# Attention and a two-axis DFT on one core: right operands in four pieces, x terms in three cycles, five weight sets during V

## The chip, the cores and the metric

The kernel runs on one core of one Trainium2 chip. The metric is the device time in microseconds of one execution. TensorE (PE) multiplies, VectorE (DVE), ScalarE (ACT) and GpSimd (POOL) work on tiles, and SyncE (SP) issues nearly all the DMA transfers, in the order of its own queue.

## The reference

The input x has 2048 rows of 640 numbers. One branch is attention with 32 heads of 20 numbers, the other is the real part of a Fourier transform along the 640 and then along the 2048; a gate mixes them row by row.

```python
qkv = (x @ wqkv).reshape(B, S, 3, H, Dh)           # S = 2048, H = 32, Dh = 20
p = softmax(einsum("bhqd,bhkd->bhqk", q, k) * Dh ** -0.5)
a = einsum("bhqk,bhkd->bhqd", p, v).reshape(B, S, D) @ wo
re, im = x @ dft_hid_re.T, x @ dft_hid_im.T        # along the 640
b = dft_seq_re @ re - dft_seq_im @ im              # along the 2048
g = sigmoid((x * gate_w).sum(-1))
out = g * a + (1 - g) * b
```

Everything is float32. Where precision asks for it, the kernel splits an operand into a high and a low part and multiplies high by high, high by low and low by high, three matmuls for one product.

## The kernel before, in words

**Stages.** First come the first projections of queries and keys and the values V: `v_pair` (L382) makes two blocks of 128 rows of V for one half of the heads, eight times for each half. It fills its tile with ones on POOL (L385), and ACT copies the two products into it; a store to the scratch buffer `v_scr` follows. Then come the other projections of queries and keys, 32 tiles (the loop at L587, `qk_pairs`), each of which stores 512 KB to `qk_scr`. Then the main loop of 1024 steps runs to the last scores; behind it come the last output tiles.

**The transform along the 640** is computed as seven products of sums of blocks (`FEATURE`, in the manner of Strassen), in two halves: 14 sets of weights, the *right operands*. POOL makes them: `load_weights` (L400) loads a half's four blocks (1600 KB), and `make_set` (L407) adds two blocks where the product has two, rounds the sum to its high part and subtracts that for its low part, on 128 x 800 numbers each; both parts are stored to `w_scr`. The sets of the first half are made during V and in the first projection tiles, those of the second half in later ones: `qk_pairs` takes one piece of such work from a list per tile. Later `load_right` (L422) fetches one set (z, the high and low part, times h, two halves of the partitions: 1600 KB in all) into a tile `wb`, of which there are two.

**The left operands** are sums of blocks of x. `load_left` (L431) loads the terms `raw` from the input `in_xh`, in the tile ring `part`, and makes five slabs out of them on POOL, one in each cycle.

**The main loop.** A string, `ORDER`, sets the order within a cycle of four steps, some 6.3 us: score products for the exponentials (e, matmul L1064, exponential on ACT L1070), score products for the maxima of a later step (m, L191, maximum on DVE L193, 43 steps ahead), 15 matmuls of filling work (F) and the products with V (B). Eight cycles are a unit (one pair of heads, one half of the queries, some 50 us); there are 32 units, and even units begin a new pair of heads, whose operands `kst`, `qst` (from `qk_scr`) and `v` are loaded at their start. The filling work of the first 56 cycles is the transform along the 640: `hid_pair` u in cycle u (matmuls L499), four pairs to a set of right operands. ACT (L508) and DVE (L509) read a pair's result, POOL (L512) adds it to an old sum, and sums which do not stay on the chip come from and go to `a_scr`, through three slots. From cycle 56 the filling work is the transform along the 2048, 3 cycles to a tile. Its left operands are parts of the matrices `in_cdft` (`load_c_first`, L662), its right operands are split from the sums (`load_a_early` L693, `make_a_early` L700, for the first of them).

**What else goes through SP.** A unit's end (`unit_end`, L718) stores the row of the sums of its exponentials (`l_scr`, L727), loads it in another shape (`lc`, L730), inverts it on DVE (L733), and sends it on (L736, L740). The maxima of a unit are stored to `m_scr` (L234) and loaded into the rows of `qst` (L240), which the scores of the next unit need.

**The order.** The instructions of each engine are in the order in which the program issues them. `at_step(i, fn)` puts a function at the start of step i of the main loop, and `flush` issues the stores that wait in a list. SP issues its transfers one behind the other: a transfer that waits (for a buffer, or for its data) holds up all those behind it.

```python
# begin(i), at the start of step i
for fn in later.pop(i, ()):
    fn()
# hid_pair: old sum of a slot, and the new one
at_step(now[0] + 4, functools.partial(sp.dma_start, old, row))
at_step(now[0] + (4 if new else 11), functools.partial(sp.dma_start, row, m if new else old))
```

Of the kernel before, what the change touches and what calls it, by code (L numbers as in the profile page):

```python
# [83 lines left out]
def f32(ap):  # L84
    return ap.bitcast(F32)
# [3 lines left out]
def mix_kernel(ctx: ExitStack, tc: tile.TileContext, xa, xh, wqk, wb, wr, cdft, wo, out):  # L89
    nc = tc.nc  # L90
    pe, act, dve, pool, sp = nc.tensor, nc.scalar, nc.vector, nc.gpsimd, nc.sync
# [20 lines left out]
    w_scr = dram.tile([SETS, 2, 64, RW], F32, name="w_scr")  # L112
# [44 lines left out]
    def v_tile():  # L157
        return work.tile([P, NS, VW], F32, name="v", bufs=2)
# [18 lines left out]
    def at_step(i, fn):  # L177
        later.setdefault(i, []).append(fn)
# [76 lines left out]
    def block(z, t):  # L255
        return proj.tile([P, ND * 512], R, name=f"x{z}{t}")
# [70 lines left out]
    def flush(keep=0):  # L327
        while len(stores) > keep:
            sp.dma_start(*stores.pop(0))
# [52 lines left out]

    def v_pair(hf, s):
        vst = v_tile().rearrange("p s e -> p (s e)").rearrange("p (a k e) -> p a k e", a=NP // 2, k=2)
        pool.memset(vst, 1.0)  # L385
        for k in range(2):
            ps = bank()
            mm_b(hf, s + k, ps, HE + 2 * hf)
            act.activation(
                vst[:, :, k, :].rearrange("p a (h e) -> p a h e", h=2)[:, :, :, :DH],  # L390
                ps[:, :HE].rearrange("p (a h e) -> p a h e", h=2, e=DH), AF.Copy)
            if hf:
                act.activation(logit[:, s + k : s + k + 1], ps[:, HE : HE + 1], AF.Copy)
        stores.append((
            v_scr[hf * (NP // 2) : (hf + 1) * (NP // 2), :, s : s + 2, :].rearrange("a p k e -> p a (k e)"),
            vst.rearrange("p a k e -> p a (k e)")))
        flush(1)


    def load_weights(hf):  # L400
        w = f32(wide.tile([P, 2, ND, BW], R, name="wb", bufs=2)).rearrange("p z d c -> p (z d c)")
        w = w[:, : 2 * RW].rearrange("p (b c) -> p b c", b=4)
        sp.dma_start(w, wr[hf])
        blocks_ = {(ri, dh): w[:, 2 * ri + dh] for ri in range(2) for dh in range(2)}
        return [(2 * n + hf, [blocks_[ri, dh] for _, dh, ri in f[1]], f[1][-1][0]) for n, f in enumerate(FEATURE)]
# [16 lines left out]
    def load_right(k):  # L422
        w = wide.tile([P, 2, ND, BW], R, name="wb", bufs=2).rearrange("p z d c -> p (z d c)")[:, : 2 * RW]
        w = w.rearrange("p (z c) -> p z c", z=2)
        for h in range(2):
            sp.dma_start(f32(w)[64 * h : 64 * h + 64], w_scr[k].rearrange("z r c -> r z c"))
        rights[k] = w.rearrange("p z (d c) -> p z d c", d=ND)

    stages = []

    def load_left(n, stage):  # L431
        terms = FEATURE[n][0]
        hi, lo = [block(z, 2 + n % 2) for z in range(2)]

        def load(q):
            c = slice(1024 * q, min(1024 * q + 1024, ND * 512))
            raws = stage(q)
            for raw, (_, th, dh) in zip(raws, terms):
                sp.dma_start(raw[:, : c.stop - c.start], xh[th, dh, :, c])
            return raws  # L440

        def slab(j, raws):
            c = slice(512 * j, 512 * j + 512)
            a, b = [raw[:, j % 2 * 512 : j % 2 * 512 + 512] for raw in raws]
            if len(terms) > 1:
                pool.tensor_tensor(a, a, b, op=ALU.add if terms[1][0] > 0 else ALU.subtract)
            split(hi[:, c], lo[:, c], a, pool, pool)

        lefts[n] = [l.rearrange("p (d c) -> p d c", d=ND) for l in (hi, lo)]
        raws = {}  # L450

        def step_(j):
            def fn():
                if j == 0:
                    raws[0], raws[1] = load(0), load(1)
                if j:
                    slab(j - 1, raws[(j - 1) // 2])
                if j == 2:
                    raws[2] = load(2)
            return fn  # L460

        return [step_(j) for j in range(ND + 1)]
# [94 lines left out]
    def load_v(p):  # L557
        vts[p] = v_tile()
        sp.dma_start(vts[p], v_scr[p])

    order = [1, ND + 1, 2, ND + 2, 3, ND + 3, 4, ND + 4]
    for s in range(0, NS, 2):
        v_pair(1, s)
        if s == 6:
            fin()
            fin = load_wqk(order[1], pool)
        if s == 0:
            sets = load_weights(0)
        if s in (4, 8, 12):
            add, finish = make_set(*sets.pop(0), *(pair_tile().rearrange("p z c -> p (z c)")[:, : RW // 2] for _ in range(2)))  # L570
            add(), finish()
        if s == 12:
            fin()
# [13 lines left out]
    for m, (n, t) in enumerate(tiles):  # L587
        qk_pairs(order[n], t, m)
        if m == 8:
            load_v(0)  # L590
            sets = load_weights(1)
            queue_sets()
        if n < 5 and t == 1:
            fin()
            if n + 3 < len(order):
                fin = load_wqk(order[n + 3], pool)
        if m == 19:
            fin()
        if m == 22:
            slabs = load_left(0, raw_stage)  # L600
        if m in (24, 26):
            flush()
            load_right((m - 24) // 2)
        if slabs:
            slabs.pop(0)()
    assert not work_
# [93 lines left out]
    def make_a_early():  # L700
        s, raw = early.pop(0)
        a = a_tile(0, s)
        split(a[:, 0], a[:, 1], raw, pool, pool)
# [248 lines left out]
    HID = 8 * len(FEATURE)  # L952
# [11 lines left out]
    for u in range(UNITS):  # L964
        k, t = LONG[u // HT], u % HT
# [18 lines left out]
    for k, tt in enumerate(PRE):  # L984
        i = 4 * tiles[2 * k]

        def load(tt=tt, i=i):
            at_step(i - 6, load_pre(tt))
# [26 lines left out]
    def end(i):  # L1015
        if i % 4 == 2:
            c = i // 4
            n, k = divmod(c, 8)
            if c < HID:
                if c % 4 == 0 and 2 <= c // 4 + 1 < SETS:  # L1020
                    at_step(i + 1, functools.partial(load_right, c // 4 + 1))
                if k == 0 and n + 1 < len(FEATURE):
                    slabs.extend(load_left(n + 1, own_stage))
                if slabs:
                    slabs.pop(0)()
                if c in (HID - 9, HID - 7, HID - 5):
                    for s in {9: (8, 0), 7: (4,), 5: (12,)}[HID - c]:
                        load_a_early(s, s + 4)
                if HID - 8 <= c:
                    at_step(i + 2, make_a_early)  # L1030
                    at_step(i + 4, make_a_early)
                if c in (HID - 4, HID - 2):
                    at_step(i + 5, load_c_first((c - HID + 4) // 2))
            if c == HID:
                at_step(i + 4, load_c(2))
        if i in LAST:
            LAST[i]()
# [195 lines left out]
```

## Time and profile before

| | |
|---|---|
| time, median of 3 runs | 1890.98 us (1884.69 to 1891.51) |
| time of the profiled execution | 1893.02 us |
| span of its trace | 1890.9 us |
| matmul instructions on PE | 17917 |
| data moved by DMA | 342.25 MB, mean 181 GB/s |
| share of the 16 DMA engines, main queue | 60.5% |

The page gives each engine's busy time, then the span in 40 slices, then groups of instructions. Its rows of groups read: line, engine, operation, output <- input, count, then busy time and mean, then the idle time just before them and what ended most of it. In the rows of waits, an engine's instruction stands before the arrow and what it waited for behind it, with total, number and longest. In rows of the timeline stand start, length, engine, line, operation and, in brackets, the idle time before and its releaser; "SPq" is a transfer that SP issues, and its length is that of the issue. In the table by stretches stand length, then the busy time (and number of instructions) of PE, its weight loads (PEld), DVE, ACT and POOL, the granted clock, the share of the 16 DMA engines, and GB/s.

The profiled execution's time is 2.1 us above the span of its trace, and 2.0 above the median.

### The profile page before, as it was taken

To read this page: it belongs to the slowest core of one execution; us is meant where nothing else is said; L and a number is where in the kernel's file an instruction comes from. 1 tells how busy PE (TensorE), PEld (TensorE's weight loads), DVE (VectorE), ACT (ScalarE), POOL (GpSimd) and SP (SyncE) were. 2 spreads that over 40 slices of the span, in tenths; PEclk is the share of its full clock that TensorE was granted. 3 is DMA by queue.
4 is the path that set the end of the run, shared out by engine and by line. 5 is a ranking of instruction groups with operands and counts; after the bars stand their busy time and mean duration, and the time that the engine had idled before them with its cause. 6 is when DMAs were issued, how large, how long until landed. Compare 5 with 4: busy or idle time off the path is not lost. (4 is left out here: it accounts for less than half of the span.)

```text
span 1890.9 us, 45912 instructions
## 1 busy us (share of the span) xinstructions
PE 1853.7 (98%) x17917; PEld 1343.0 (71%) x17917; DVE 1455.3 (77%) x2420; ACT 1237.0 (65%) x2378; POOL 1304.7 (69%) x1106
## 2 busy tenths in 40 slices
PE   9999899989799999999999999999999999999998
PEld 8988777757476767777777767667676767776666
DVE  4157388878687888888888888788888888889953
ACT  4233267767576667677776777667676766777785
POOL 1488735473765999566689989967879987834444
PEclk9999999999899999999999999999999999999999
DMA  7867875777677585545657575647476655532214
GB/s 231 211 232 277 265 207 142 176 217 194 191 205 205 178 249 158 158 131 158 190 155 232 173 242 179 205 124 200 152 229 208 192 182 178 169 96 80 63 50 157
DMA packets 194684, 342.25 MB, mean 181 GB/s; under 512 B 54191, under 2 KB 107567, under 8 KB 194211
## 3 DMA queue, kind: packets, MB, share of 16 engines
q1 hardware_dynamic: 193507, 337.35, 60.5%
q0 software_dynamic: 960, 1.97, 0.5%
q8 instruction: 141, 2.31, 0.5%
q14 instruction: 76, 0.62, 0.1%
HBM read 257.79 MB, written 81.28 MB: 179 GB/s over the span
## 5 line engine op out<-in xcount | busy, mean ns | idle before, releaser
L193 DVE TENSOR_REDUCE mx<-ps 128x1 f32<-128x512 f32 x2048 | 1299.9, 685 | 245.8 <-PE ps L191 219.7
L1070 ACT ACTIVATE p<-ps 128x512 f32<-128x512 f32 x2048 | 1088.1, 598 | 450.7 <-PE ps L191 222.9
L191 PE MATMUL ps<-kst,qst 60*128 60x512 f32 x2048 | 780.6, 415 | 10.4 <-DMA qk_scr<-p 6.0
L1064 PE MATMUL ps<-qst,kst 62*128 62x512 f32 x2048 | 698.7, 416 | 13.7 <-DMA qst<-m_scr 13.7
L794 PE MATMUL yp<-x,part 64*128 64x320 f32 x5376 | 645.1, 306 | 0.0
L794 PEld LDWEIGHTS yp<-x,part 64*128 64x128 f32 x5376 | 582.5, 186 | 7.5 <-POOL part L131 0.4
L1064 PEld LDWEIGHTS ps<-qst,kst 62*128 62x128 f32 x2048 | 335.1, 186 | 238.4 <-DVE mx L193 128.8
L713 PE MATMUL av<-p,v 128*21 128x512 f32 x4096 | 497.8, 602 | 0.0
L191 PEld LDWEIGHTS ps<-kst,qst 60*128 60x128 f32 x2048 | 369.9, 185 | 23.8 <-ACT p L369 6.4
L131 POOL TENSOR_TENSOR part<-raw,part 128x1024 fp32r<-128x1024 f32 (+3 forms) x134 | 297.0, 2216 | 11.3 <-ACT part L128 1.1
L713 PEld LDWEIGHTS av<-p,v 128*21 128x21 f32 x4096 | 95.8, 100 | 211.2 <-issue 210.1
L130 POOL CAST part<-raw 128x1024 fp32r<-128x1024 f32 (+2 forms) x127 | 125.1, 985 | 134.4 <-PE yp L794 118.3
L499 PE MATMUL yp<-wb,x 64*128 64x320 f32 x1680 | 212.4, 312 | 3.8 <-ACT raw L508 3.8
L655 POOL TENSOR_TENSOR raw<-raw,raw 128x1024 f32<-128x1024 f32 x78 | 187.1, 2399 | 36.7 <-DMA raw<-in_cdft 16.6
L499 PEld LDWEIGHTS yp<-wb,x 64*128 64x128 f32 x1680 | 184.6, 191 | 7.3 <-ACT raw L508 4.2
L131 POOL TENSOR_TENSOR x<-araw,x 128x320 fp32r<-128x320 f32 x96 | 83.9, 874 | 7.7
L865 PE MATMUL yp<-x,part 64*128 64x320 f32 x720 | 87.4, 309 | 0.0
L512 POOL TENSOR_TENSOR x<-x,raw 128x640 f32<-128x640 f32 x40 | 62.4, 1560 | 30.0 <-DVE raw L509 21.3
L882 POOL TENSOR_TENSOR x<-x,m 128x320 f32<-128x320 f32 x30 | 26.2, 874 | 82.3 <-DVE m L877 71.6
L865 PEld LDWEIGHTS yp<-x,part 64*128 64x128 f32 x720 | 75.7, 185 | 2.7
L688 POOL TENSOR_TENSOR araw<-araw 128x320 f32<-128x320 f32 x80 | 70.0, 875 | 0.4 <-DMA araw<-a_scr 0.4
L363 PE MATMUL yp<-x,part 64*128 64x512 f32 x480 | 62.3, 390 | 1.1 <-POOL part L131 1.1
(106 smaller groups left out, 1364.6 us busy)
## 6 DMA issues: line engine op xcount, KB each, us to landing
raw<-in_cdft SPq DMA_DIRECT2D x189, 512.0 KB
araw<-a_scr SPq DMA_DIRECT2D x176, 160.0 KB
wb<-w_scr SPq DMA_DIRECT2D x28, 800.0 KB
qk_scr<-p SPq DMA_DIRECT2D x40, 512.0 KB
kst<-qk_scr SPq DMA_DIRECT2D x90, 160.0 KB
qst<-qk_scr SPq DMA_DIRECT2D x90, 160.0 KB
part<-in_xh SPq DMA_DIRECT2D x22, 512.0 KB
yt<-y_scr SPq DMA_DIRECT2D x64, 160.0 KB
```

The costliest lines, as they stand in the source:

```text
L130: e1.tensor_copy(dst1, src)
L131: e2.tensor_tensor(dst2, src, f32(dst1), op=ALU.subtract)
L191: pe.matmul(ps, q[b : b + KROWS, qt * P : (qt + 1) * P], k[b : b + KROWS, kc * 512 : (kc + 1) * 512], start=True, stop=True)
L193: return lambda: dve.tensor_reduce(mx[n][:, h, qt, kc : kc + 1], ps, axis=AX.X, op=ALU.max)
L499: pe.matmul(ps[z], lefts[n][a][r, d, k * P : k * P + P], rights[2 * n + hf][r, b, d], start=done_ == 0, stop=done_ == 3 * ND - 1)
L655: pool.tensor_tensor(raws[0], raws[0], raws[1], op=ALU.add if PRODUCTS[n][0][1][0] > 0 else ALU.subtract)
L688: pool.tensor_tensor(raws[0], raws[0], raws[1], op=ALU.add if PRODUCTS[n][1][1][0] > 0 else ALU.subtract)
L713: pe.matmul(av[32 * j : 32 * j + DH + 1, :], v[:, kt, h * (DH + 1) : (h + 1) * (DH + 1)], pp[qc][:, h, :], start=kt == 0, stop=kt == NS - 1)
L794: pe.matmul(yp[h][:, :HE], c[r, cz, cs], a[r, az], start=s == 0 and z == 0, stop=s == NS - 1 and z == 2)
L865: pe.matmul(yp[h][:, :HE], o[r, oz, d], wos[d, hf][r, wz], start=d == 0 and z == 0, stop=d == ND - 2 and z == 2)
L1064: pe.matmul(pt, k[b : b + KROWS + 2, kt * P : (kt + 1) * P], q[b : b + KROWS + 2, qc * 512 : (qc + 1) * 512], start=True, stop=True)
L1070: act.activation(pts[n, kt, qc][:, h], pt, AF.Exp, scale=float(DH) ** -0.5)
```

## The change

There are five edits. They leave the order of instructions on PE and ACT as it was.

1. The tiles of V of the second half are filled by DVE instead of POOL (8 fills).
2. `load_right` no longer issues its two transfers of 800 KB, but gives back four of 400 KB (64 partitions x 1600 numbers). Before the main loop they are issued one per projection tile, in the tiles 20 to 27, instead of two in each of the tiles 24 and 26 (there behind a `flush` of the stores). In the main loop they stand at the steps i+1, i+4, i+7 and i+10 instead of both at i+1.
3. `load_left` loads its second piece of terms at its second call, a cycle later, so that three pieces go out in three cycles.
4. Five sets of weights instead of three are made during V, and the second half's blocks are loaded in projection tile 4 instead of 8.
5. `make_a_early` is called once instead of twice in the last two of the eight cycles in which it stands, and twice at the end of cycle 56's second step.

```diff
 def v_pair(hf, s):
-        pool.memset(vst, 1.0)
+        (dve if hf else pool).memset(vst, 1.0)
...
 def load_right(k):
-        for h in range(2):
-            sp.dma_start(f32(w)[64 * h : 64 * h + 64], w_scr[k].rearrange("z r c -> r z c"))
         rights[k] = w.rearrange("p z (d c) -> p z d c", d=ND)
+        return [functools.partial(sp.dma_start, f32(w)[64 * h : 64 * h + 64, z], w_scr[k, z]) for z in range(2) for h in range(2)]
...
 # load_left
-                if j == 0:
-                    raws[0], raws[1] = load(0), load(1)
+                if j < 2:
+                    raws[j] = load(j)
...
-        if s in (4, 8, 12):
+        if 4 <= s <= 12:
             add, finish = make_set(...)
             add(), finish()
...
 # loop over the projection tiles m
         if m == 8:
             load_v(0)
+        if m == 4:
             sets = load_weights(1)
             queue_sets()
...
-        if m in (24, 26):
-            flush()
-            load_right((m - 24) // 2)
+        if m in (20, 24):
+            chunks = load_right((m - 20) // 4)
+        if 20 <= m < 28:
+            chunks.pop(0)()
...
 # end(i), at the end of each cycle's second step
                 if c % 4 == 0 and 2 <= c // 4 + 1 < SETS:
-                    at_step(i + 1, functools.partial(load_right, c // 4 + 1))
+                    for q, fn in enumerate(load_right(c // 4 + 1)):
+                        at_step(i + 1 + 3 * q, fn)
...
                 if HID - 8 <= c:
                     at_step(i + 2, make_a_early)
+                if HID - 8 <= c < HID - 2:
                     at_step(i + 4, make_a_early)
...
             if c == HID:
+                make_a_early()
+                make_a_early()
                 at_step(i + 4, load_c(2))
```

The first place is SP's queue at the start of unit 4, where a new pair of heads, new terms of x and a new set of right operands are loaded (`wb<-w_scr` is the right operands, `part<-a_scr` an old sum, `part<-in_xh` terms of x). Before, from the middle of that stretch:

```order
L1003 DMA kst_92<-qk_scr 20x4x512
L426 DMA wb<-w_scr 64x2x1600 x2
L1003 DMA kst_92<-qk_scr 20x4x512 x2
L1003 DMA part<-a_scr 128x640
L559 DMA v<-v_scr 128x672
L1003 DMA kst_92<-qk_scr 20x4x512
L727 DMA l_scr<-o 4x512
L1003 DMA kst_92<-qk_scr 20x4x512
L1003 DMA qst_94<-qk_scr 20x4x512 x2
L1003 DMA part<-a_scr 128x640
L1003 DMA qst_94<-qk_scr 20x4x512
L730 DMA lc<-l_scr 128x16
```

And in the changed kernel, from the store of the sums' row on (its line numbers are larger by one):

```order
L728 DMA l_scr<-o 4x512
L1004 DMA wb<-w_scr 64x1600
L438 DMA part<-in_xh 128x1024 x2
L1004 DMA kst_92<-qk_scr 20x4x512
L1004 DMA qst_94<-qk_scr 20x4x512 x2
L1004 DMA wb<-w_scr 64x1600
L1004 DMA part<-a_scr 128x640
L1004 DMA qst_94<-qk_scr 20x4x512
L731 DMA lc<-l_scr 128x16
L438 DMA part<-in_xh 128x512 x2
L1004 DMA qst_94<-qk_scr 20x4x512 x2
L1004 DMA wb<-w_scr 64x1600
```

The set stood whole ahead of the sums' row. Now one piece of it stands ahead of that row, the second right behind it, the third behind two terms of x and three loads of heads, and the last one behind three more loads of heads, the load of the row in its other shape and two more terms of x.

The second place is SP's queue ahead of the store of a unit's maxima (`m_scr<-m`), in unit 3. Before:

```order
L1003 DMA part<-a_scr 128x640
L1003 DMA a_scr<-part 128x640
L426 DMA wb<-w_scr 64x2x1600 x2
L1003 DMA part<-a_scr 128x640
L1003 DMA a_scr<-part 128x640
L736 DMA r_scr<-lc 128x16
L1003 DMA part<-a_scr 128x640
L234 DMA m_scr<-m 128x64
L1003 DMA a_scr<-part 128x640
L240 DMA qst_94<-m_scr 1x32x32 x4
```

The same stretch in the changed kernel:

```order
L1004 DMA a_scr<-part 128x640
L1004 DMA wb<-w_scr 64x1600
L1004 DMA part<-a_scr 128x640
L1004 DMA a_scr<-part 128x640
L1004 DMA wb<-w_scr 64x1600
L737 DMA r_scr<-lc 128x16
L1004 DMA wb<-w_scr 64x1600
L1004 DMA part<-a_scr 128x640
L234 DMA m_scr<-m 128x64
L1004 DMA a_scr<-part 128x640
L240 DMA qst_94<-m_scr 1x32x32 x4
L1004 DMA wb<-w_scr 64x1600
```

The whole set stood ahead of one load and one store of sums; now one piece stands there, two more stand ahead of the store of the maxima, and the last behind the loads of the maxima.

The third place is POOL during V, where `v` is the tile that is filled with ones, `p<-wb` and `p<-p` the sum, the high and the low part of a set. Before:

```order
L385 MEMSET v 128x672 x5
L410 TENSOR_TENSOR p<-wb 128x800
L130 CAST p<-p 128x800
L131 TENSOR_TENSOR p<-p 128x800
L385 MEMSET v 128x672 x2
L410 TENSOR_TENSOR p<-wb 128x800
L130 CAST p<-p 128x800
L131 TENSOR_TENSOR p<-p 128x800
L385 MEMSET v 128x672 x2
L130 CAST p<-wb 128x800
L131 TENSOR_TENSOR p<-wb,p 128x800
L131 TENSOR_TENSOR part<-raw,part 128x640
```

In the changed kernel, from the last fills of the first half on:

```order
L385 MEMSET v 128x672 x2
L410 TENSOR_TENSOR p<-wb 128x800
L130 CAST p<-p 128x800
L131 TENSOR_TENSOR p<-p 128x800
L410 TENSOR_TENSOR p<-wb 128x800
L130 CAST p<-p 128x800
L131 TENSOR_TENSOR p<-p 128x800
L130 CAST p<-wb 128x800
L131 TENSOR_TENSOR p<-wb,p 128x800
L410 TENSOR_TENSOR p<-wb 128x800
L130 CAST p<-p 128x800
L131 TENSOR_TENSOR p<-p 128x800
```

The fills between the sets are gone, and another set follows behind these rows, ahead of the split of `part`.

## The prediction

> **What bounds the kernel now.** First the page's busy times, then who TensorE (PE) waited for over the whole span.
>
> ```profile
> PE 1853.7 (98%) x17917; PEld 1343.0 (71%) x17917; DVE 1455.3 (77%) x2420; ACT 1237.0 (65%) x2378; POOL 1304.7 (69%) x1106
> PE ps L1064 <- DMA qst<-m_scr: 13.7, 3, 7.3
> PE ps L191 <- DMA qk_scr<-p: 6.0, 1, 6.0
> PE ps L191 <- DVE mx L193: 4.4, 3, 2.2
> PE yp L499 <- ACT raw L508: 3.8, 1, 3.8
> PE yp L363 <- POOL part L131: 1.1, 1, 1.1
> ```
>
> PE is the bound: 37 us idle in 1890.9, and the change leaves its instructions and those of ScalarE (ACT) in their order. So only a wait of PE, or its clock, can move the time. Five rows hold the large waits (total, times, longest). I call them **A** (1.1, weights late, at 192.7), **B** (6.0, at 230.6, with 0.8 just ahead of it), **C** and **E** (5.7 and 7.3, a unit's maxima late, at 389.7 and 501.6), **D** (2.2, at 477.5) and **F** (3.8, at 609.1). Behind each the clock runs at half rate. The table by stretches, from each resumption to full clock (length, PE, PEld, DVE, ACT, POOL, clock, DMA share, GB/s):
>
> ```profile
> 236.60:245.80 9.20, 9.20 (x51) 8.12 (x52) 6.48 (x10) 4.91 (x9) 2.10 (x2) 0.51 0.77 257
> 395.36:399.30 3.94, 3.94 (x18) 0.91 (x18) 0.00 (x0) 1.42 (x3) 0.21 (x1) 0.52 0.71 223
> 481.00:485.00 4.00, 4.00 (x23) 0.82 (x22) 2.39 (x5) 1.41 (x3) 3.45 (x4) 0.57 0.70 218
> 508.86:515.20 6.34, 6.34 (x30) 2.67 (x32) 1.10 (x2) 3.06 (x6) 2.30 (x2) 0.50 0.59 161
> 614.00:618.00 4.00, 4.00 (x33) 4.00 (x31) 2.52 (x5) 2.56 (x5) 3.84 (x6) 0.57 0.02 8
> ```
>
> Length times the missing clock gives 4.5, 1.9, 1.7, 3.2 and 1.7 us. So A costs 1.1, B 6.8 + 4.5 = 11.3, C 7.6, D 3.9, E 10.5, F 5.5: **39.9 us** are all that can be won. D shows that 2.2 us of idleness is enough to halve the clock.
>
> The Trainium skill (TensorE: Matmul & The Clock Gate, Part 1: The HAM clock gate) gives the half clock after an idle window of about 3.4 us. C and E agree; D does not, and the measurement decides. By the page D would cost 2.2 only, and the sum below would be 1.7 us higher.
>
> **C and E: the right operands.** SyncE's queue (SP) ahead of C, and PE's resumption:
>
> ```profile
> 373.80 1.25 SPq L426 DMA_DIRECT2D wb<-w_scr  x2
> 377.52 0.38 SPq L1003 DMA_DIRECT2D a_scr<-part  x1
> 387.82 0.32 SPq L1003 DMA_DIRECT2D part<-a_scr  x1
> 388.23 1.06 SPq L234 DMA_DIRECT2D m_scr<-m  x1
> 391.15 2.83 SPq L240 DMA_DIRECT2D qst<-m_scr  x4
> 395.36 0.89 PE L1064 MATMUL ps<-qst,kst 62*128 62x512 f32 x2 [5.69 <-DMA qst<-m_scr]
> SPq L1003 <- DMA a_scr<-part: 13.2, 3, 8.7
> ```
>
> The chain: two right loads, 1600 KB, go ahead of a store of a sum (377.52). The next load into that slot has to wait for that store, SP stands 8.7 us, and the store of the maxima behind it goes 8 us late. In a quiet unit the way is short:
>
> ```profile
> 279.01 0.33 SPq L234 DMA_DIRECT2D m_scr<-m  x1
> 280.51 2.83 SPq L240 DMA_DIRECT2D qst<-m_scr  x4
> 349.00:353.00 4.00, 4.00 (x46) 3.34 (x48) 3.94 (x7) 3.29 (x8) 0.00 (x0) 1.00 1.00 207
> ```
>
> The third row is a stretch with little but right data in flight: all 16 DMA engines busy at 207 GB/s. So a whole set (1638 kB) takes 7.9 us and a piece 2.0. After the change one piece instead of four lies ahead of the slot's store, and SP's stand shrinks from 8.7 to about 2.7 us. The store of the maxima then goes at about 382 instead of 388.23. From there to PE it took 395.36 - 388.23 = 7.1 us, or 5.8 after the quiet 1.5 us store; PE wants the rows at 389.7. That fits, or misses by 1 us since the third piece now precedes the store. I leave 1.0 us of each: C gives 6.6, E 9.5.
>
> **B.** Here the loads stand in the projections' end:
>
> ```profile
> 212.02 1.37 SPq L426 DMA_DIRECT2D wb<-w_scr  x2
> 218.45 1.24 SPq L426 DMA_DIRECT2D wb<-w_scr  x2
> 235.44 0.63 ACT L128 ACTIVATE p<-p 128x512 fp32r<-128x512 f32 x1 [7.07 <-DMA qk_scr<-p]
> ```
>
> Two sets are 15.8 us of DMA between 212 and 230, among stores of 512 KB a tile; ACT then waits 7.07 us for a store to free its buffer, and PE for ACT. After: one piece a tile over eight tiles, four tiles earlier, and the last weight set is made four tiles earlier too. A tile, from one pair of halves to the next:
>
> ```profile
> 207.10 1.77 PE L363 MATMUL yp<-x,part 64*128 64x512 f32 x14
> 210.78 1.77 PE L363 MATMUL ps<-x,part 64*128 64x512 f32 x14
> ```
>
> It lasts 3.7 us. A piece takes 2.0 and a store of 524 kB, at the 257 GB/s of the first row of the table by stretches, another 2.0: 4.0, a lag of 0.3 a tile, which the four tiles behind the last piece give back; only the three tiles with x loads stay fuller. I take 10.3 of 11.3. **A** (1.1) goes with the earlier weight sets, as POOL then has four tiles without them.
>
> **D** is DVE waiting for the sums' row, whose store lay behind x loads and the whole set:
>
> ```profile
> SPq L730 <- DMA l_scr<-o: 10.3, 1, 10.3
> 478.83 0.25 DVE L733 RECIPROCAL lc<-lc 128x16 f32<-128x16 f32 x1 [2.44 <-DMA lc<-l_scr]
> ```
>
> Now two x loads (1024 KB) and three pieces move behind that store: over 8 us less ahead of it, against 2.44 needed. D gives 3.9.
>
> **What the change adds.** The fourth piece now stands behind most of the loads of a new pair of heads, at the start of units 2, 4 and 6, and must land before the fourth cycle after. Unit 4, with the same lists for units 2 and 6:
>
> ```profile
> 475.20 1.54 SPq L1003 DMA_DIRECT2D qst<-qk_scr  x3
> 474.88 0.31 PE L499 MATMUL yp<-wb,x 64*128 64x320 f32 x2
> 447.00:484.00 37.00, 34.82 (x330) 22.94 (x330) 30.21 (x52) 24.92 (x50) 18.40 (x15) 0.96 0.90 222
> 339.00:369.00 30.00, 30.00 (x300) 20.81 (x298) 26.20 (x45) 22.07 (x44) 11.24 (x9) 1.00 0.90 202
> 562.00:595.00 33.00, 32.57 (x320) 22.39 (x322) 28.53 (x49) 24.10 (x48) 20.54 (x25) 1.00 0.90 208
> ```
>
> In unit 4 the queue up to and with piece four holds 11 head loads (160 KB), 6 x loads (2560 KB), 3 of sums (960), v (336) and the set (1600): 7216 KB, 7.39 MB. At 222 GB/s that is 33.3 us, at 222 / 0.90 29.9. From the unit's start at 446.3, with 1.5 us to land, it is there at 477.7 to 481.1, while pair 36 begins at 474.88 (second row): late by 2.8 to 6.2, taken as 5.2, and the clock 2.0: **+7.2**. The first row agrees: two of those three loads stand ahead of piece four. Unit 2: 5.75 MB, 25.7 to 28.5 us from 338.4, there at 365.6 to 368.4, needed at about 367.0: up to 1.4 late, taken as 1.3 with 0.5 of clock: **+1.8**. Unit 6: 6.73 MB from 558.4, there at 589.0 to 592.3, needed at 589.4: 0 to 2.9 late, with clock up to 4.4.
>
> **F** hangs on unit 6:
>
> ```profile
> 595.12 0.85 SPq L670 DMA_DIRECT2D wb<-in_cdft  x2
> 603.58 2.40 POOL L674 TENSOR_TENSOR wb<-wb 128x1024 f32<-128x1024 f32 x1 [9.07 <-DMA wb<-in_cdft]
> 610.87 1.53 POOL L512 TENSOR_TENSOR x<-x,raw 128x640 f32<-128x640 f32 x1
> 612.43 0.44 ACT L508 ACTIVATE raw<-yp 128x320 f32<-128x320 f32 x1 [4.56 <-POOL x L512]
> ```
>
> POOL makes the first sequence part late, since its data is late; the addition that ACT needs comes after it. The moved operands stand behind that addition in both orders, so the third edit neither removes nor adds anything here. But a PE that waits at pair 52 gives this load as much time: what unit 6 adds, F loses. I take **0** for the two together (from -5.5 to +4.4).
>
> **The weight sets in V.** POOL gets two sets more and eight fills less:
>
> ```profile
> L410 POOL TENSOR_TENSOR p<-wb 128x800 f32<-128x800 f32 x2 | 3.9, 1928 | 0.0
> L385 POOL MEMSET v<- 128x672 f32 x9 | 5.9, 657 | 15.9 <-DMA v_scr<-v 15.2 <-ACT logit L393 0.6
> 95.00:107.00 12.00, 12.00 (x84) 11.68 (x84) 0.00 (x0) 3.52 (x13) 8.95 (x9) 1.00 0.80 225
> ```
>
> A set of two terms is about 4.7 us (1.9 + 0.9 + 1.9), of one 2.8: 7.5 more, 8 x 0.66 = 5.3 less. DVE has no fill of this size in the trace; it was idle for 12 of 12 us there (its figure in the third row is 0.00), so even at 657 ns, or at twice that, it is hidden: 0. What is queued behind a fill that waits for its store is DVE's splitting of weights (0.8 us), wanted over 10 us later. PE was busy throughout, and the five banks of PSUM hold two and a half pairs of tiles ahead of a late drain.
>
> **Sum:** -1.1 - 10.3 - 6.6 - 9.5 - 3.9 + 7.2 + 1.8 + 0 = -22.4. From the profiled execution's 1893.0: 1870.6, 2.0 above the median's footing. I say **1871**.
>
> **The rivals.**
> - *No piece is late* (chance 0.18). For: the DMA share is 0.90, not 1, and small loads use part of the engines, so that pieces may pass beside them. All but 2 to 4 us of 39.9 go: about 1856.
> - *The new pairs' starts give it back* (0.14): pieces late by 4, 8 and 5 us with 7 of clock instead of 9.0 in all: 1870.6 + 15 = 1886. For it: in the trace unit 4's last loads were issued only at 475.2.
> - *Each piece pays a fixed price* (0.06). A store of 32 KB took 1.5 us from issue to its reader (279.01 to 280.51), so two more transfers a set cost up to 3.0; where the queue is full (units 2, 4, 6) 9 us, with clock 12: 1883. Against it: in the row at 207 GB/s the engines show share 1.00, no gap between transfers. The Trainium skill (DMA: Bandwidth & Descriptors, Anatomy of one DMA and Bandwidth) has such a rule, about 2.0 us fixed and batches of 1 MiB or more; by it two more transfers would cost 4.0 us a set, and the sum be about 1887.
> - *C and E stay* (0.07): pieces two and three still delay the store of the maxima by as much, since SP runs ahead and issues them together. Against: 8.7 us shrink by six. 1870.6 + 16.1 = 1887.
> - *Slower* (0.06): every one of twelve sets comes late, as the fourth piece goes out behind the loads of the maxima. In the quiet unit those end at 283.3; a piece issued then lands by 286.8 (2.0 + 1.5), some 3 us ahead of its pair. It decides from a landing 5.5 us after issue instead of 3.5: 12 x (2.3 + 1.2 of clock) = 42, so 1893 - 31.4 + 42 = 1904.
>
> **How the numbers follow.** The forecast keeps 0.49 (its own range 1862 to 1880). Half a per cent of 1891 is 9.5 us, about what a measurement of this kernel can tell from no change: faster ends at 1881.5. The forecast and the first rival are faster, with a quarter of the second and half of the third: 0.73. Same: the rest of those and the fourth: 0.20. Slower: 0.07. The range, 1856 to 1889, reaches from the first rival over the second, third and fourth.
>
> **What would show it.** C and E: no wait of PE for qst<-m_scr above 1.5 us, SP's wait for a_scr<-part under 4. B: ACT's wait for qk_scr<-p under 3. D: DVE not waiting for lc. New: PE L499 waiting for wb<-w_scr at the fourth cycle of units 2, 4, 6, unit 4 worst. A new wait of PE in V, or at units 1, 3, 5, would make it wrong.

## The result, and the profile after

The changed kernel takes 1880.69 us (median of 7 runs, 1879.48 to 1887.19), the kernel before 1887.38 (median of 7, 1884.69 to 1891.51). The ratio is 0.9964, with a 95% interval of 0.9947 to 0.9980. The profiled executions stand 12.3 us apart (1893.02 and 1880.69), since the one of before lies above its median. The forecast was 1871, or 22 us less than the profiled execution of before. By the profiled executions a little over half of that came, by the medians (6.7 us) less than a third.

First, who PE waited for, in the changed kernel:

```profile
PE yp L498 <- DMA wb<-w_scr: 23.4, 4, 8.8
PE ps L294 <- DVE x L288: 1.5, 1, 1.5
PE ps L191 <- DVE mx L193: 1.4, 1, 1.4
PE ps L191 <- ACT p L369: 0.5, 1, 0.5
```

Every large wait of before is gone: no row for `qst<-m_scr`, none for `qk_scr<-p`, none for ACT's late read. One wait stands in their place, for the right operands, four times and 23.4 us. The timeline of PE has it at these places (the two at 468 and 477 are both in pair 36):

```profile
361.52 1.43 PE L498 MATMUL yp<-wb,x 64*128 64x320 f32 x7 [5.72 <-DMA wb<-w_scr]
...
468.23 0.63 PE L498 MATMUL yp<-wb,x 64*128 64x320 f32 x1 [4.83 <-DMA wb<-w_scr]
477.67 1.43 PE L498 MATMUL yp<-wb,x 64*128 64x320 f32 x7 [8.80 <-DMA wb<-w_scr]
...
583.80 1.43 PE L498 MATMUL yp<-wb,x 64*128 64x320 f32 x7 [4.01 <-DMA wb<-w_scr]
```

These are the fourth cycles after the starts of units 2, 4 and 6, where the prediction looked for them; but 13.6 us in unit 4 instead of 5.2. The stretches behind them, and the one from unit 4's start to the landing (columns as before):

```profile
434.30:477.70 43.40, 29.77 (x289) 19.90 (x287) 26.57 (x45) 22.16 (x44) 19.90 (x16) 0.88 0.88 193
361.52:371.00 9.48, 9.48 (x82) 7.70 (x84) 6.45 (x11) 5.45 (x11) 8.07 (x7) 0.83 0.64 184
477.67:487.00 9.33, 9.33 (x81) 7.52 (x83) 6.35 (x11) 5.35 (x11) 7.81 (x7) 0.83 0.57 165
583.80:593.00 9.20, 9.20 (x65) 7.31 (x67) 5.00 (x9) 4.04 (x8) 0.78 (x1) 0.66 0.78 279
```

The clock at 0.83 over 9.4 us costs 1.6 us more in units 2 and 4, at 0.66 it costs 3.1 in unit 6.

PE's matmuls are the same 17917 in the same order in both kernels, so each can be set against its twin. The start of a matmul less that of its twin in the kernel before, at moments of the kernel before, gives what each stretch won or lost (us). Of the other columns, which are experiments below, "all at once" is the first, "units at once" the second, "x later" the one with the x terms two cycles later, and the last one those two together:

```
moment of before      after   all at once   units at once   x later   at once, x later
190 (V ends)           -0.2       +0.3          +0.9          +0.1         -0.4
205 (A passed)         -1.7       -1.1          -0.6          -1.3         -1.8
250 (B)               -12.0      -11.4         -10.9         -11.6        -11.9
385 (unit 2)           -4.4      -11.5         -10.9          -9.6        -12.0
430 (C)               -12.0      -11.7         -14.1         -16.8        -19.5
486 (unit 4, D)        -0.2       -8.8         -14.2         -10.7        -23.6
540 (E)               -10.6      -11.8         -20.2         -21.1        -27.1
606 (unit 6)           -3.9      -12.3         -20.7         -12.5        -27.5
625 (F)                -9.5      -16.4         -24.3         -18.1        -33.2
1889 (end)            -12.9      -21.1         -27.9         -19.1        -34.8
```

In the first column A and B won 11.8, C 7.6, E 10.4 and F 5.6; units 2 and 6 lost 7.5 and 6.4 (taken right at their waits, without the drift that the rows of the table hold), unit 4 with D 11.8. The 3.4 us behind 625 were won further on, 1.8 of them at a late row of sums at 1207 which no edit was aimed at; they were not followed up.

Each column is one execution. The five kernels of the table's columns are the same up to the main loop and lie within 1.1 us at 250, so a difference of 1 us between columns tells nothing.

### The profile page after: what moved, and what is told of

It reads as the page before. It is cut to its first block, busy times and chain, and to the rows that moved or that the text cites. A ratio compares the mean times of both kernels' runs of the same rounds, so it can differ in the third digit from the quotient of the medians.

```text
span 1878.8 us, 45939 instructions
## 1 busy us (share of the span) xinstructions
PE 1845.9 (98%) x17917; PEld 1344.8 (72%) x17917; DVE 1459.4 (78%) x2428; ACT 1237.4 (66%) x2378; POOL 1300.1 (69%) x1098
## 5 line engine op out<-in xcount | busy, mean ns | idle before, releaser
L714 PE MATMUL av<-p,v 128*21 128x512 f32 x4096 | 492.5, 596 | 0.0
L191 PEld LDWEIGHTS ps<-kst,qst 60*128 60x128 f32 x2048 | 368.5, 185 | 14.2 <-DVE mx L193 1.6
L498 PE MATMUL yp<-wb,x 64*128 64x320 f32 x1680 | 214.7, 314 | 23.4 <-DMA wb<-w_scr 23.4
L511 POOL TENSOR_TENSOR part<-part,raw 128x640 f32<-128x640 f32 x16 | 25.0, 1563 | 53.5 <-DMA part<-a_scr 34.7
```

Of the source, the lines that this page charges most:

```text
L191: pe.matmul(ps, q[b : b + KROWS, qt * P : (qt + 1) * P], k[b : b + KROWS, kc * 512 : (kc + 1) * 512], start=True, stop=True)
L498: pe.matmul(ps[z], lefts[n][a][r, d, k * P : k * P + P], rights[2 * n + hf][r, b, d], start=done_ == 0, stop=done_ == 3 * ND - 1)
L511: pool.tensor_tensor(old, old, m, op=ALU.add if sign > 0 else ALU.subtract)
L714: pe.matmul(av[32 * j : 32 * j + DH + 1, :], v[:, kt, h * (DH + 1) : (h + 1) * (DH + 1)], pp[qc][:, h, :], start=kt == 0, stop=kt == NS - 1)
```

## The experiments

**Is it the place of the pieces?** The pieces of a set together again:

```diff
-                        at_step(i + 1 + 3 * q, fn)
+                        at_step(i + 1, fn)
```

> The changed kernel, but the four pieces of a set stand together at step i+1, as the whole set stood before. Theory P (the place of the last piece behind the loads of a new pair of heads makes it late): PE waits under 1 us for wb<-w_scr, the 29.6 us of unit 2, 4 and 6 (7.5 + 15.7 + 6.4 with the clock) go, and C (7.6), E (10.4), D (3.9) and F (5.6) come back: 1880.7 - 29.6 + 27.5 = 1879, between 1874 and 1884. Rival S (a set in four transfers of 64 partitions lands more slowly wherever it stands): waits for wb<-w_scr of 10 us and more stay, and C and E come back as well: over 1889.

Measured: 1872.81 us (ratio to before 0.993, 0.9909 to 0.995). No wait for `wb<-w_scr` is left; instead:

```profile
PE ps L1069 <- DMA qst<-m_scr: 9.7, 2, 5.3
PE ps L191 <- DVE mx L193: 4.9, 2, 3.9
```

C and E are back with 9.7 us of waiting (13.0 before), and D with 3.9. F is not (1.2 us), and the time is 1 us below the range of theory P. So four transfers for a set cost nothing by themselves, and rival S falls. The kernel is 8 us faster than with the pieces spread in every set: spreading loses more at three units' starts than it wins at two units' middles. (C's store of the maxima stands in the second half of unit 2, not in unit 3, as the change has it; its rows are for unit 3.)

**At once only where a unit starts, spread in its middle:**

```diff
-                        at_step(i + 1 + 3 * q, fn)
+                        at_step(i + 1 + (3 * q if k else 0), fn)
```

> The changed kernel, but in the sets that are loaded at a unit's start the four pieces stand together at i+1; in the sets of a unit's middle they stay spread. Theory P: the waits for wb<-w_scr of units 2, 4, 6 go (-29.6), C and E stay away, D may come back (+3.9) and F too (+5.6): 1851 to 1861. Rival S: the waits go down by half at most: 1866 or more. Rival X (the x terms, a cycle later, are what the pieces wait behind): waits of some 10 us stay: 1863 or more.

Measured: 1865.78 us (0.9902, 0.9883 to 0.9922). No wait for `wb<-w_scr`, as theory P had it; but the time is 5 us above its range, since C and E did not stay away:

```profile
PE ps L1069 <- DMA qst<-m_scr: 4.9, 2, 2.5
PE ps L191 <- DVE mx L193: 3.4, 2, 2.0
```

Without the late piece C wins 3.2 us and not 7.6, E 6.0 and not 10.4 (third column). The rest of their gain in the changed kernel was no gain: PE, held by the late piece in the same unit, came to the rows of the maxima late enough to find them there. In the changed kernel the loads of the rows for C go out at 378.40, and PE comes to them at 385.09:

```profile
378.40 2.80 SPq L240 DMA_DIRECT2D qst<-m_scr  x4
...
385.09 0.47 PE L1069 MATMUL ps<-qst,kst 62*128 62x512 f32 x2
```

Here the loads go out 1.3 us earlier (377.07), but PE is ready 6.3 us earlier (at 378.79, and works from 381.26). D (2.0) had been hidden in the same way. SP's queue ahead of C here:

```profile
368.19 0.45 SPq L1004 DMA_DIRECT2D wb<-w_scr  x1
368.74 0.55 SPq L737 DMA_DIRECT2D r_scr<-lc  x1
369.33 0.45 SPq L1004 DMA_DIRECT2D wb<-w_scr  x1
371.05 0.33 SPq L1004 DMA_DIRECT2D part<-a_scr  x1
371.43 0.42 SPq L234 DMA_DIRECT2D m_scr<-m  x1
371.95 0.38 SPq L1004 DMA_DIRECT2D a_scr<-part  x1
377.07 2.81 SPq L240 DMA_DIRECT2D qst<-m_scr  x4
```

The store of the maxima goes out 5.9 us earlier than before (388.23 less the 10.9 by which all is ahead is 377.3): the 6 us that the prediction worked out. But it needs 5.6 us to the loads instead of 2.9 in C before, with two pieces right ahead of it. These are not the whole reason: with the same two ahead of it the store needs 3.1 us in the changed kernel (375.26 to 378.40).

**X terms as before** (`load_left` loads both first pieces in its first call again):

```diff
-                if j < 2:
-                    raws[j] = load(j)
+                if j == 0:
+                    raws[0], raws[1] = load(0), load(1)
```

> The changed kernel with its third edit undone: both first pieces of x terms are loaded in a unit's first cycle. Theory P: as many bytes lie ahead of the last piece as in the changed kernel, so it is as late: waits for wb<-w_scr of 20 to 26 us in all; D may come back (+3.9): 1879 to 1886. Rival X: the waits go down to under 12 us, and the time to 1866 or less.

Measured: 1878.56 us (0.9962, 0.9941 to 0.9983), not told apart from the changed kernel. Waits for `wb<-w_scr` are 18.3 us, 10.1 of them in unit 4. So the x terms' third cycle is a part of unit 4's lateness (13.6 there with it), but neither theory's number is met whole (20 to 26 and under 12): P is nearer.

**A set in two transfers of 800 KB at i+1 and i+10:**

```diff
-        return [functools.partial(sp.dma_start, f32(w)[64 * h : 64 * h + 64, z], w_scr[k, z]) for z in range(2) for h in range(2)]
+        return [functools.partial(sp.dma_start, f32(w)[64 * h : 64 * h + 64], w_scr[k].rearrange("z r c -> r z c")) for h in range(2)]
...
-                        at_step(i + 1 + 3 * q, fn)
+                        at_step(i + 1 + 9 * q, fn)
```

(In the projections these two stand in the first two of the four tiles of a set.)

> The changed kernel with a set in two transfers of 800 KB, at i+1 and at i+10, the places of the first piece and of the last. Theory P: what stands at i+10 is as late or later (it is twice as large, 2 us): waits for wb<-w_scr of 22 to 32 us: 1879 to 1890. Rival N (each transfer has a price, so that half as many of them land sooner): the waits halve, 1864 to 1870.

Measured: 1886.28 us (1.0008, 0.9994 to 1.0023), waits for `wb<-w_scr` 30.6 us, 14.2 in unit 4. Theory P is met: what counts is the last place and the size of what stands there, not the number of transfers.

**How far behind may the last piece stand?** At a unit's start one step and two steps apart, instead of at once or three:

```diff
-                        at_step(i + 1 + (3 * q if k else 0), fn)
+                        at_step(i + 1 + (3 if k else 1) * q, fn)
```

(and 2 for that 1 in the other)

> The kernel of the second experiment, but at a unit's start the four pieces stand one step apart (i+1 to i+4) instead of at once; three steps apart in a unit's middle, as before. Theory Q (the piece's own place: a step is 1.57 us, the last piece at i+10 leaves four steps, 6.3 us, until its pair, and lands 9 to 11 us after its issue; at i+4 ten steps, 15.7 us, are left): no wait for wb<-w_scr above 1 us, 1862 to 1868. Rival B2 (all that stands between the pieces counts: the queue is full from the first piece on): unit 4 waits by 3 us or more, 1870 or more.

> The same with the pieces two steps apart at a unit's start (i+1, i+3, i+5, i+7). Theory Q: seven steps, 11.0 us, are left behind the last one, against 9 to 11 us of landing and some 5 us by which SP lags in unit 4: a wait of 0 to 6 us there, 0 to 2 in units 2 and 6: 1864 to 1874. Rival B2: as late as three apart, waits of 20 us or more, 1880 or more.

Measured: 1873.19 us (0.9898, 0.9861 to 0.9934; single runs from 1866 to 1877) and 1876.82 (0.9926, 0.9903 to 0.995). One step apart, no row for `wb<-w_scr` is left; two steps apart:

```profile
PE yp L498 <- DMA wb<-w_scr: 4.8, 2, 4.2
```

The waits for the right operands by spacing (0, 1, 2, 3 steps) are 0, 0, 4.8 and 23.4 us, the last with the pieces of the middle in the same places. Theory Q is met by the waits, and rival B2 falls by them, though one step apart its time came (1870 or more). The times are above what Q gave, for other reasons. One step apart, the row `lc` of the reciprocal comes later in units 4 and 6 (DVE waits 4.5 and 4.2 us for it), and the largest wait is D's:

```profile
468.52 0.79 PE L191 MATMUL ps<-kst,qst 60*128 60x512 f32 x1 [4.24 <-DVE mx L193]
```

Two steps apart, C, E and F still cost 2.8, 2.1 and 2.4 us of waiting.

**The x terms two cycles later, pieces spread in every set:**

```diff
-                if slabs:
+                if slabs and k >= 2:
                     slabs.pop(0)()
```

> The changed kernel, pieces spread in every set, with the x terms of a unit loaded two cycles later (cycles 2 to 4 of a unit in place of 0 to 2), so that 2560 KB no longer stand ahead of the fourth piece. Theory B (bytes ahead of the last piece, and the rate at which they move): at 193 GB/s that is 13.6 us, so it lands in time: waits for wb<-w_scr of 2 us at most in all, D goes, and C and E give what they gave in the second experiment: 1859 to 1867. Rival R (pieces between small loads are slow, whatever stands ahead): waits for wb<-w_scr of 12 us or more stay: over 1871.

Measured: 1874.36 us (0.9926, 0.9906 to 0.9946), waits for `wb<-w_scr` 14.7 us: rival R's number, though not for its reason.

```profile
357.72 0.85 PE L498 MATMUL yp<-wb,x 64*128 64x320 f32 x7 [1.57 <-DMA wb<-w_scr]
...
465.95 1.43 PE L498 MATMUL yp<-wb,x 64*128 64x320 f32 x7 [7.18 <-DMA wb<-w_scr]
...
575.50 1.43 PE L498 MATMUL yp<-wb,x 64*128 64x320 f32 x7 [5.70 <-DMA wb<-w_scr]
```

Units 2 and 4 wait 1.6 and 7.2 us instead of 5.7 and 13.6, so the bytes ahead count. Unit 6 loads no x terms in any of the kernels, which the expectation overlooked; its piece is late all the same (4.0 us in the changed kernel, 5.7 here), so x terms are not needed for that. And in unit 4 the first two x terms still go out ahead of the fourth piece:

```profile
448.73 1.33 SPq L438 DMA_DIRECT2D part<-in_xh  x2
451.78 1.00 SPq L1004 DMA_DIRECT2D qst<-qk_scr  x2
454.41 0.45 SPq L1004 DMA_DIRECT2D wb<-w_scr  x1
```

From issue to use the piece takes 11.5 us (454.41 to 465.95), with 1024 KB of x in flight ahead of it.

**The same two cycles, and one cycle, with the pieces at once at a unit's start** (the edit above with `k >= 2` and `k >= 1`, put on the kernel of the second experiment):

> The kernel of the second experiment with the x terms two cycles later. Theory B: the row of the sums has neither x terms nor their transfers beside it, so D's 2.05 us and the clock behind it go: 1861 to 1864. Rival K: the x terms now collide with the store and loads of the maxima, whose wait (C, E, 2.4 us each) grows: 1867 to 1875.

> The kernel of the second experiment with the x terms one cycle later (cycles 1 to 3). Theory B: D shrinks by half or goes, C and E as they are: 1861 to 1866. Rival K: C and E grow by 1 to 3 us: 1867 to 1871.

Measured: 1857.94 us (0.9845, 0.9826 to 0.9865) and 1857.75 (0.9855, 0.983 to 0.988), the fastest of all and both below theory B's ranges. Two cycles later, PE's waits in the main loop are:

```profile
PE ps L1069 <- DMA qst<-m_scr: 4.7, 2, 4.2
PE ps L191 <- DVE mx L193: 2.2, 1, 2.2
```

D is gone (from 472 to 486 this kernel wins 4 us over before; the 2.2 is another one, at 1174), C too; E's wait of 4.2 is larger than in the second experiment, as rival K had it, but in one place only. That C goes when the x terms move was in neither theory, and why it does was not followed up. One cycle later C is gone too and E is 1.3 us; 0.4 us of waiting stay at D's place, and 2.5 us come 5 us behind it.

**The third piece of a unit's middle behind the loads of the maxima:**

```diff
-                        at_step(i + 1 + (3 * q if k else 0), fn)
+                        at_step(i + ((1, 4, 10, 10)[q] if k else 1), fn)
```

> The kernel with a unit's first set at once (the second experiment), where in the set of a unit's middle the third and fourth piece both stand at i+10, behind the loads of the maxima, instead of at i+7 and i+10. Theory M (what is left of C and E, 2.47 and 2.42 us, is pieces two and three ahead of the store of the maxima, which takes 4.7 us from its issue to the loads): that falls to under 3 us, C and E to under 1 us each: 1865.8 - 5 to 7 with the clock: 1858 to 1862. Rival L (the two last pieces, issued some 3 us ahead of the next unit, land too late for its first pair, in six units): waits for wb<-w_scr of 1 to 3 us each: 1866 to 1880.

Measured: 1866.71 us (0.9893, 0.9875 to 0.9912), as the second experiment. The waits of theory M go down, but three others take their place:

```profile
379.61 0.59 PE L1069 MATMUL ps<-qst,kst 62*128 62x512 f32 x2 [1.31 <-DMA qst<-m_scr]
...
384.37 0.85 PE L498 MATMUL yp<-wb,x 64*128 64x320 f32 x7 [1.33 <-DMA wb<-w_scr]
...
466.59 0.79 PE L191 MATMUL ps<-kst,qst 60*128 60x512 f32 x1 [4.65 <-DVE mx L193]
...
494.59 0.85 PE L498 MATMUL yp<-wb,x 64*128 64x320 f32 x7 [1.34 <-DMA wb<-w_scr]
```

C's wait falls from 2.47 to 1.31 and E's goes. Two pairs wait 1.3 us for their right operands, of the six that rival L named. The largest item is D, which grows from 2.05 to 4.65: PE comes to it 1.5 us earlier than in the second experiment, and the row it needs comes 1.1 us later. By the matmuls' times the stretch of D loses 3.9 us against the second experiment, and those of C and E win 1.0 and 2.3.

Two more kernels of the experiments below (the first two sets loaded as before; the fifth edit undone) do the same as the second experiment's from unit 2 to the end of unit 4. In them C's wait is 1.62 and 3.71 us (2.47 in the second experiment), D's 2.61 and 3.03 (2.05), E's 3.35 and 1.64 (2.42). So these waits differ by 1 us or so from one execution to the next, and the gains of C and E without a late piece (3.2 and 6.0) are no surer than that.

**What did away with B?** On the second experiment's kernel, first the two sets ahead of the main loop are loaded as before; then also the fills and the weight sets are put back:

```diff
-        if m in (20, 24):
-            chunks = load_right((m - 20) // 4)
-        if 20 <= m < 28:
-            chunks.pop(0)()
+        if m in (24, 26):
+            flush()
+            for fn in load_right((m - 24) // 2):
+                fn()
...
-        (dve if hf else pool).memset(vst, 1.0)
+        pool.memset(vst, 1.0)
...
-        if 4 <= s <= 12:
+        if s in (4, 8, 12):
...
-        if m == 4:
+        if m == 8:
             sets = load_weights(1)
```

> The kernel of the second experiment with the first two sets loaded as before: each whole at one place, in the tiles 24 and 26, behind a flush of the stores; the weight sets stay early. Theory as predicted (the loads' place and size make ACT wait for its buffer): PE's wait of 6.0 us at the end of the projections comes back with its clock: 1865.8 + 8 to 11 = 1874 to 1877. Rival (the last weight set, made four tiles later, was what filled the queue): it stays away, 1865 to 1868.

> The same with the first and fourth edits undone too, so that up to the main loop all is as in the kernel before, and only the main loop is changed. The weight sets' edits are worth 1.4 to 1.6 us (A), as predicted: both A and B come back, 1865.8 + 11.8 = 1877 to 1879. Rival: the earlier weight sets also carry a part of B: more than 3 us between this kernel and the one with the two loads alone.

Measured: 1869.37 us (0.9915, 0.9891 to 0.9939) and 1875.79 (0.9959, 0.9939 to 0.9979). PE's wait at the projections' end, in the first of them:

```profile
230.35 0.54 PE L191 MATMUL ps<-kst,qst 60*128 60x512 f32 x1 [3.06 <-ACT p L369]
```

and in the second:

```profile
192.66 1.44 PE L363 MATMUL yp<-x,part 64*128 64x512 f32 x10 [0.79 <-POOL part L131]
...
235.96 0.79 PE L191 MATMUL ps<-kst,qst 60*128 60x512 f32 x1 [5.26 <-ACT p L369]
```

With the loads put back half of B's wait returns; with the weight sets put back nearly all of it, and most of A's. By the matmuls' times, reckoned as in the table, B won 10.3 us in the second experiment, 6.5 with the loads put back, and 2.3 with fills and sets put back too; A (190 to 205) won 1.4, 1.4 and 0.3. So in B the loads carry some 3.8 us and fills and sets together 4.2; the two were not put back apart. The last 2.3 belong to no edit: that kernel is the kernel before up to the main loop, and they are a difference between two executions, as large as which the error of these shares may be. The rival of the second expectation holds: the earlier sets, or the fills with them, also carry a part of B. The profiled execution of this last kernel took 10 us more than its median, so only its part up to the main loop is used.

**The fifth edit undone** on the second experiment's kernel (two parts a cycle in all eight cycles, none at cycle 56):

> The kernel of the second experiment with the fifth edit undone: two parts a cycle are made in all eight cycles, as before. As the prediction had it, the edit does nothing: ACT's late read at pair 55 (1.7 us of PE) stays as it is: 1865 to 1867. Rival: the edit took F away (3.8 us and 1.7 of clock before, 1.7 now): F comes back to 3.5 us and more, 1868 to 1871.

Measured: 1867.59 us (0.9899, 0.9878 to 0.9921), not told apart from 1865.78. Two rows of PE:

```profile
591.50 0.47 PE L498 MATMUL yp<-wb,x 64*128 64x320 f32 x2 [0.81 <-ACT raw L507]
...
619.57 0.79 PE L795 MATMUL yp<-x,part 64*128 64x320 f32 x6 [1.64 <-POOL part L131]
```

F's wait is as small without the edit (0.81) as with it (1.67; 3.85 before), so the edit does not act there. But a wait of 1.64 us comes at 619.6, which neither the kernel before nor the one with the edit has; with the clock it costs some 3.5 us in this trace. So the edit may spare that wait; with one execution of each this is not shown.

## Why the prediction was wrong

It was wrong in size: 1871 where 1880.7 came, and of 22 us to be won 7 (by the medians) or 12 (by the profiled executions) came.

**The step that failed** is "From the unit's start at 446.3, with 1.5 us to land, it is there at 477.7 to 481.1 [...] late by 2.8 to 6.2, taken as 5.2, and the clock 2.0: +7.2", and the same working for unit 2 (+1.8). The two terms were 9.0 in the sum; they measured 7.5 in unit 2 and 15.7 in unit 4 (11.8, with D's 3.9 in it): 23.2. Unit 6 and F, taken as 0, came to +0.8 (+6.4 and -5.6). The mechanism of the late piece and its places were right; the terms were too small by 14.2 us.

Two things were off in that working, and a simpler one was left out. SP's queue in unit 4 of the changed kernel:

```profile
438.32 0.48 SPq L1004 DMA_DIRECT2D wb<-w_scr  x1
...
444.42 0.48 SPq L1004 DMA_DIRECT2D wb<-w_scr  x1
446.76 1.35 SPq L438 DMA_DIRECT2D part<-in_xh  x2
...
455.81 0.45 SPq L1004 DMA_DIRECT2D wb<-w_scr  x1
...
463.64 0.83 SPq L438 DMA_DIRECT2D part<-in_xh  x2
465.23 1.62 SPq L1004 DMA_DIRECT2D qst<-qk_scr  x2
468.21 0.45 SPq L1004 DMA_DIRECT2D wb<-w_scr  x1
469.06 0.27 SPq L1004 DMA_DIRECT2D qst<-qk_scr  x1
```

- **Bytes.** From the unit's start to the landing 8.38 MB moved, not 7.39: the stores of sums and outputs and the load issued just behind the piece share the engines, and were left out. At the rate used, 222 GB/s, that is 4.5 us. Moved in that time (434.30 to 477.70), by the trace's account of DMA:

```profile
DMA packets 3364, 8.38 MB, mean 193 GB/s; under 512 B 557, under 2 KB 557, under 8 KB 3358
```

- **Rate.** It moved at 193 GB/s, not 222: 5.7 us more. The row of 222 had been measured with the x loads in one burst and the set behind it; before, the same kinds of loads (446.3 to 482) went at 215. With the x terms as before and the pieces spread (third experiment) it is 210, and 39.6 us until the piece is there. So a rate read in one kernel was carried to another order of loads; how much of the difference the order makes, and how much single executions differ, is open (last section). With both, the 33.3 us of the prediction become 43.5 (43.4 in the trace). In unit 2 it was the same: 6.49 MB at 185 GB/s, 35.1 us, instead of 5.75 at 202, 28.5.
- **Slack.** The piece issued at 468.21 was used at 477.67, 9.5 us later; the third one, issued at 455.81, at 468.23, 12.4 later. In unit 2 the last piece took 11.2 us (350.36 to 361.52), in unit 6 9.0. The prediction's 3.5 was an estimate from a quiet unit, in its rival Slower. A step is 1.57 us, so the place i+10 leaves 6.3 us to the next set's first pair, less than a landing in a full queue takes even if SP does not lag. That sum from the steps alone, which needs no rate, gives a late piece in each of the three units; the prediction did not make it. The two spacings show it: with 11.0 us left behind the last piece the waits are 4.8 us in all, with 15.7 there are none.

The Trainium skill (DMA: Bandwidth & Descriptors, Queues, rings and completion order) says that each DMA engine takes a queue's descriptors in ring order. The 9.5 and 12.4 us agree with that: a late piece waits for what is in flight ahead of it, however small it is itself.

**Point by point, the rest.** *A* was right: -1.1 forecast, 1.4 measured. *B* was right in size (10.3 both times) but not in cause: the forecast put it on the loads' place, and the experiments show some 3.8 us for that and 4.2 for the fills and the earlier weight sets, of which it had named the last set without a share. *C and E* (6.6 and 9.5) measured 7.6 and 10.4, but for the wrong reason: without the late piece they are 3.2 and 6.0. The shift of the store of the maxima was right (6 us); what was too low, at 1.0 us, is what its way to the loads grows by with two pieces right ahead: it is 5.6 us in the second experiment, 2.9 before. That the two terms came out near their forecast is luck: the late pieces covered what was left of these waits. *D* (3.9) was wrong and hidden: the row came later, not earlier, as DVE's timeline of the changed kernel shows,

```profile
470.21 0.25 DVE L734 RECIPROCAL lc<-lc 128x16 f32<-128x16 f32 x1 [5.82 <-DMA lc<-l_scr]
```

5.82 us of waiting against 2.44 before, all of it in the time in which PE stood for its right operands. Taking the x terms away from it made D go. *F* went by 5.6 and not through the fifth edit, as said (the prediction calls it the third); why its data comes some 2 us sooner in all variants was not settled. The *fills and sets in V* cost nothing: at 190 us the changed kernel is 0.2 us ahead.

Of the rivals, the second (units' starts give it back, 1886) was nearest in mechanism: it took 4, 8 and 5 us of lateness, and 5.7, 13.6 and 4.0 came. The first (no piece late) is what the second experiment built, 1865.8, not 1856, since C, D and E stay in part. A price per piece is not seen, neither 3.0 nor 4.0 us a set: four transfers at once show no wait. The 39.9 us that the prediction had as all that can be won left out one more wait with a half clock behind it, 1.8 us at 1207.

## What to carry to other kernels

A transfer that is spread out to get out of others' way must still be issued a full landing ahead of its use, and the landing is that of the busy queue in which it will stand (here 9 to 12 us), not that of a quiet one (estimated at 3.5). When several waits go at once and a new one appears, ask which of the old ones the new one merely covers; undo the new one to see them. Spread only where a queue is short of room for something urgent: here the middle of a unit, not its start.

## What the runs showed of the hardware that was not expected

The same kinds of loads moved at 229 GB/s in one kernel and 193 in another: in unit 4 with the set at once, and with its pieces between small loads. The stretch from the unit's start on in the second experiment's kernel, and there the stretches behind C and E:

```profile
432.20:468.00 35.80, 33.75 (x332) 23.34 (x332) 29.73 (x51) 25.04 (x50) 18.01 (x15) 0.99 0.88 229
381.26:386.00 4.74, 4.74 (x25) 1.45 (x27) 0.15 (x1) 1.99 (x5) 0.00 (x0) 0.64 0.92 255
489.83:495.00 5.17, 5.17 (x32) 2.23 (x34) 0.77 (x2) 2.75 (x6) 0.33 (x1) 0.67 0.86 251
```

In both kernels the DMA engines were 0.88 busy, so the difference is in the time that the packets take and not in idle engines. How much of it is the order's is not settled: over the first 35.8 us of unit 4 the changed kernel moved 201 GB/s, the second experiment 228, but the first one, with the same order in that unit, 212.

Behind waits of 2.47 and 2.42 us (C and E of the second experiment) the clock was 0.64 and 0.67 over 4.7 and 5.2 us, a loss of 1.7 us each; behind 5.72 and 8.80 us it was 0.83 over 9.4, a loss of 1.6: the length of a wait does not set the loss behind it. What the loss depended on here is where the half clock lies. In unit 2 of the changed kernel the granted clock was 0.50 from 357.9 to 364.7, more than half of that while PE still waited (until 361.52); behind C in the second experiment it was 0.50 from 381.7 to 385.2, all of it while PE worked (from 381.26).
